# Two attention layers mixed by a gate: first loads from three queues, and the last rows' work shared among four engines

## The chip, the cores and the metric

The kernel runs on one core of one Trainium2 chip. The metric is the device time of one launch in microseconds (us); before the change it is 2832.03 us, the median of three runs (2831.45 to 2834.38). A core has a matrix engine (TensorE; PE in the profile, with PEld its weight loads), a vector engine (DVE), a scalar engine (ACT), a general engine (Pool) and a queue engine (SP) that only issues transfers. ACT and Pool can issue transfers too, in the order of their other work.

## The reference

Two attention layers read the same input and are mixed row by row by a gate. Layer A has 32 heads with keys and values of their own; layer B has 32 query heads and one shared key and value. S is 2048, D is 576, a head is 18 wide.

```python
x = A_x
g = _sigmoid((x * gate_w).sum(-1, keepdims=True))
a = _A_ref(x, A_wqkv, A_wo)      # full attention, 32 heads
b = _B_ref(x, B_wq, B_wk, B_wv, B_wo)   # 32 query heads, one key and value
return g * a + (1 - g) * b
```

Each layer is softmax(q k^T / sqrt(18)) v for every head, the heads side by side, times an output matrix of 576x576. So the output is one product: the 64 heads' rows, each divided by its softmax sum and multiplied by its gate, times the two output matrices stacked (1152x576).

## The kernel before

Numbers that need float32 precision are split into a high and a low part (`split`: a rounding copy, then a subtraction), and a product is made as high x high + high x low + low x high.

**First stage.** The input, transposed, comes in eight chunks `xs` of 256 columns (`load_x`), each by three transfers (`load5`: 512 KB and twice 64 KB). The projection weights come in 14 blocks `wst` of 128 columns (`load_w`, 256 KB and twice 32 KB). Before the change all of these are issued by SP in this order: block 0, chunks 0 to 3, block 1, chunks 4 to 7, blocks 2 to 5. A transfer uses one of eight semaphores in turn (eight more for Pool's queue), and its issue waits until the transfer that used it before has landed. ACT and DVE split each chunk (lines 210 to 212) and each weight block (lines 126 and 127); `project` multiplies on PE (line 147), and writes the results to DRAM (`qkh` from ACT's queue, `qkl` from Pool's). Blocks 0 and 1 are projected as chunks arrive, the others in `project_rest`.

**Main stage.** A loop over steps T gives every engine a hand-written order: for each of 64 heads and 16 blocks of keys, scores on PE (line 377), exponential on ACT (line 384), the weighted sum of values on PE into `acc` (line 391), and the row maxima of the heads to come on DVE (lines 342 to 351). Other work is pulled in at given steps: the normalising of finished rows (`normalise`, nine tiles of 128 rows) and the output product (`out_proj`, three parts, each 16 tiles of rows `st_` times two halves `hf` of 288 columns), which adds each half-tile into `oacc` on DVE (line 515; the first part is copied by ACT, line 513). A half-tile takes one of four PSUM buffers `pm`.

**The end.** The ninth tile of rows holds 110 rows and is normalised with `at_end`: four chunks of 512 columns, each a multiplication, a rounding copy and a subtraction on DVE (lines 447, 116, 118), left in `qs` and `ksb` for the third `out_proj`. The last head's 18 rows get a way of their own, `last_out`: ACT copies `acc` to `oe` and rounds it to `oh` (lines 536, 114), DVE makes the low part `ol`; 12 transfers stack `oh`, `oh` and `ol` into `qs[2]` (54 rows); PE transposes the sums and DVE makes `r` from them (lines 548 to 552). Then come the half-tiles of the third `out_proj` that are left (`pull(10 ** 9)`), and at last, for each of 16 tiles, two products of the stacked rows (line 558), each scaled by `r` and added to `oacc` by one DVE instruction (line 561), and a store of the tile to `out` (288 KB) by SP. SP's and all other transfers go through the helper on line 49.

The order at the end is this:

```python
    tail = last_out()
    next(tail)
    pull(10 ** 9)
    run(tail)
```

Of the kernel before, what the change touches and what calls it, by code (L numbers as in the profile page):

```python
# [8 lines left out]
F32 = mybir.dt.float32  # L9
F32R = mybir.dt.float32r  # L10
BF16 = mybir.dt.bfloat16
AF = mybir.ActivationFunctionType
OP = mybir.AluOpType
# [29 lines left out]
def gated_mix_kernel(ctx: ExitStack, tc: tile.TileContext, xT, wall, wv, wo, out):  # L43
    nc = tc.nc
    P = 128
# [71 lines left out]
        if l is not None:  # L117
            eng_l.tensor_tensor(l, src, h.bitcast(F32), op=OP.subtract)

    def load5(t, src):  # L120
        dma(t[:, 0:4, :], src[0:512, :].rearrange("(k p) m -> p k m", p=P))
        dma(t[0:64, 4, :], src[512:576, :])
        dma(t[64:128, 4, :], src[512:576, :])

    def split_w(st, w, eng_l):
        nc.scalar.activation(w["h"], st, AF.Copy)
        eng_l.tensor_tensor(w["l"], st, w["h"].bitcast(F32), op=OP.subtract)

    def load_w(mt):
        st = wpool.tile([P, NKT, P], F32, name="wst", bufs=6)  # L130
        load5(st, wall[mt])
        return st

    def prep_w(st):
# [61 lines left out]

    WV = []
    with tc.tile_pool(name="xs", bufs=6, side="right") as xsp:
        W = [load_w(0)]
        XS = []  # L200

        def load_x(c):
            XS.append(xsp.tile([P, NKT, 256], F32, name="xs"))
            load5(XS[c], xT[:, 256 * c:256 * c + 256])

        def split_x(c):
            xs = XS[c]
            cs = slice(c * 256, (c + 1) * 256)
            xh = X["h"][:, :, cs]
            nc.scalar.activation(xh, xs, AF.Copy)  # L210
            nc.vector.tensor_tensor(X["l"][:, :, cs], xs[:, 0:4], xh[:, 0:4].bitcast(F32), op=OP.subtract)
            nc.vector.tensor_tensor(xh[64:128, 4], xs[64:128, 4], xh[64:128, 4].bitcast(F32), op=OP.subtract)

        for c in range(4):
            load_x(c)
        W.append(load_w(1))
        for c in range(4, 8):
            load_x(c)
        for mt in range(2, 6):
            W.append(load_w(mt))  # L220
        WP = [prep_w(W.pop(0))]
        for c in range(2):
            split_x(c)
        WP.append(prep_w(W.pop(0)))
        for c in range(4):
            if c < 3:
                split_x(2 * c + 2)
                split_x(2 * c + 3)
            keep = project(0, c, WP[0])
            project(1, c, WP[1])  # L230
            shared_v(*keep)
# [64 lines left out]
    L = {("kd", 0): kdb}  # L296
# [120 lines left out]
    def normalise(t, at_end=False):  # L417

        u0 = 0 if t == 0 else last_head(t - 1) + 1
        u1 = min(last_head(t) + 1, NU - 1)  # L420
        rows = min(P, DH * (NU - 1) - P * t)
        n = (u1 - u0) * 16
        sm = L["work"].tile([P, P], F32, name="sm", bufs=1)
        dma(sm[:n, :], sum_d[u0:u1, :].rearrange("h (s f) -> (h s) f", f=P))
        gt = L["work"].tile([P, P], F32, name="gt", bufs=1)
        dma(gt[:n, :], gu_d[u0:u1, :].rearrange("h (s f) -> (h s) f", f=P))
        yield
        yield
        nc.vector.reciprocal(sm[:n, :], sm[:n, :])
        (nc.vector if at_end else nc.gpsimd).tensor_tensor(sm[:n, :], sm[:n, :], gt[:n, :], op=OP.mult)  # L430
        yield
        dma(r_d[u0:u1, :].rearrange("h (s f) -> (h s) f", f=P), sm[:n, :])
        yield
        ot = OT.pop(t)
        R = L["work"].tile([P, S], F32, name="R", bufs=1)
        r0 = P * t
        while r0 < P * t + rows:
            u = r0 // DH
            n = min(DH * (u + 1), P * t + rows) - r0
            dma(R[r0 - P * t:r0 - P * t + n, :], r_d[u:u + 1, :].to_broadcast([n, S]))  # L440
            r0 += n
        yield
        if at_end:
            L["end"] = {"h": qs[1], "l": L["ks"][2]}
            for c in range(4):
                cs = slice(512 * c, 512 * c + 512)
                nc.vector.tensor_tensor(ot[:rows, cs], ot[:rows, cs], R[:rows, cs], op=OP.mult)
                split(ot[:rows, cs], L["end"]["h"][:rows, cs], L["end"]["l"][:rows, cs], nc.vector, nc.vector)
            return
        for c in range(4):  # L450
            cs = slice(512 * c, 512 * c + 512)
            h = L["work"].tile([P, 512], F32R, name="oh", bufs=1)
            l = L["work"].tile([P, 512], F32R, name="ol", bufs=1)
            nc.gpsimd.tensor_tensor(ot[:rows, cs], ot[:rows, cs], R[:rows, cs], op=OP.mult)
            yield
            split(ot[:rows, cs], h[:rows], l[:rows], nc.gpsimd, nc.gpsimd)
            yield
            yield
            dma(on_d[0][P * t:P * t + rows, cs], h[:rows])
            dma(on_d[1][P * t:P * t + rows, cs], l[:rows])  # L460
            yield

    WO = {}

# [12 lines left out]
    def out_proj(t0, rows, first=False):  # L477

        nt = len(rows)
        oacc = L["oacc"]  # L480
        O = {}

        def load(q):
            for x, y in enumerate("hl"):
                if "end" in L:
                    O[q, y] = L["end"][y][:, 256 * q:256 * q + 256].rearrange("p (t s) -> p t s", t=1)
                    continue
                t = L["pool"].tile([P, nt, 256], F32R, name=f"oi{y}", bufs=2)
                dma(t, on_d[x][P * t0:P * (t0 + nt), 256 * q:256 * q + 256]
                    .rearrange("(t p) s -> p t s", p=P))  # L490
                O[q, y] = t

        load(0)
        yield
        w = WO[t0]
        for q in range(8):
            if q < 7:
                load(q + 1)
            o = {y: O[q, y] for y in "hl"}
            for s2 in range(2):  # L500
                st_ = 2 * q + s2
                for hf in range(2):
                    fp = ps_m.tile([P, 512], F32, name="pm")
                    n = 0
                    for a, b in PRODS:
                        for t, r in enumerate(rows):
                            nc.tensor.matmul(fp[:, 0:288], o[b][:r, t, s2 * P:(s2 + 1) * P],  # L507
                                             w[a][:r, t, 288 * hf:288 * hf + 288],
                                             start=(n == 0), stop=(n == 3 * nt - 1))
                            n += 1  # L510
                    dst = oacc[:, st_, 288 * hf:288 * hf + 288]
                    if first:
                        nc.scalar.activation(dst, fp[:, 0:288], AF.Copy)
                    else:
                        nc.vector.tensor_tensor(dst, fp[:, 0:288], dst, op=OP.add)  # L515
                    yield
# [17 lines left out]
    def last_out():  # L534
        oe = L["work"].tile([P, 512], F32, name="oe", bufs=1)
        nc.scalar.activation(oe, acc, AF.Copy)
        oh = L["work"].tile([P, 512], F32R, name="oh", bufs=1)
        ol = L["work"].tile([P, 512], F32R, name="ol", bufs=1)
        split(oe, oh, ol, nc.scalar, nc.vector)
        stk = qs[2]  # L540
        for j in range(4):
            cs = slice(512 * j, 512 * j + 512)
            dma(stk[0:18, cs], oh[32 * j:32 * j + 18, :])
            dma(stk[18:36, cs], oh[32 * j:32 * j + 18, :])
            dma(stk[36:54, cs], ol[32 * j:32 * j + 18, :])
        pt = ps_m.tile([P, 512], F32, name="pm")
        for c in range(4):
            nc.tensor.transpose(pt[:, P * c:P * c + P], oe[:, P * c:P * c + P], ident)
        r = L["work"].tile([P, 16], F32, name="rl")
        nc.vector.reciprocal(r.rearrange("p (j c) -> p c j", c=4),  # L550
                             pt.rearrange("p (c j d) -> p c j d", c=4, d=32)[:, :, :, 18])
        nc.vector.tensor_tensor(r, r, L["g"], op=OP.mult)
        oacc = L["oacc"]
        yield
        for st_ in range(16):
            for hf in range(2):
                ps = ps_m.tile([P, 512], F32, name="pm")
                nc.tensor.matmul(ps[:, 0:288], stk[0:54, st_ * P:st_ * P + P],
                                 L["wl"][0:54, 288 * hf:288 * hf + 288], start=True, stop=True)
                dst = oacc[:, st_, 288 * hf:288 * hf + 288]  # L560
                nc.vector.scalar_tensor_tensor(dst, ps[:, 0:288], r[:, st_:st_ + 1], dst,  # L561
                                               op0=OP.mult, op1=OP.add)
            dma(out[st_ * P:(st_ + 1) * P, :], oacc[:, st_, :])


    NSTEP = 16 * NU
# [80 lines left out]
        run(slow.pop(0))  # L647
    tail = last_out()
    next(tail)
    pull(10 ** 9)  # L650
    run(tail)

# [33 lines left out]
```

## Time and profile before

| | us |
|---|---|
| median of three runs | 2832.03 (2831.45 to 2834.38) |
| the profiled execution | 2830.23 |
| its span | 2828.1 |
| PE busy | 2801.4 (99%) |
| ACT busy | 2447.0 (87%) |
| DVE busy | 2371.8 (84%) |
| POOL busy | 207.6 (7%) |

The span runs from the first to the last instruction of the profiled execution, which took 2.13 us more than that. Busy time is the time in which an engine worked on instructions; issues of transfers, waits and register work don't count, except that Pool's own issues do. In a row of the timeline stand start, length, engine, line, operation, output and inputs, and how many instructions were merged; brackets give the idle time before it and what ended it. `SPq` is the issuing side of SP: the length of such a row is the time to issue, not to move the data. The matrix engine's clock is given as a share of full speed.

### The profile page before, as it was taken

The page shows a single profiled execution, that of the slowest core. Times are in us where ns is not written, and L with a number is a line of the kernel's source. Part 1 is how long each engine was busy: PE and PEld are TensorE (multiplying, and loading weights), DVE is VectorE, ACT ScalarE, POOL GpSimd, SP SyncE. Part 2 cuts the span into 40 slices and gives each one's busy share as a digit, 9 for nine tenths or more (in the row PEclk, how much of TensorE's full clock was granted, in tenths as well). Part 3 has the DMA queues.
Part 4 walks back from the last instruction along what each step waited for, and adds up shares of the span by engine and source line. Part 5 has one row for each costly group of instructions (what it writes and reads, how often), then busy time and mean ns, then how long its engine had stood idle before and what let it go on. Part 6 is the DMA issues. An engine that isn't in the chain of part 4 may idle for free.

```text
span 2828.1 us, 58626 instructions
## 1 busy us (share of the span) xinstructions
PE 2801.4 (99%) x22628; PEld 1289.3 (46%) x22628; DVE 2371.8 (84%) x4461; ACT 2447.0 (87%) x4832; POOL 207.6 (7%) x364
## 2 busy tenths in 40 slices
PE   7999999999999999999999999999999999999999
PEld 5888443343433433434434444444444444345554
DVE  3346999999999999999999888888888888998765
ACT  3331999999999999999999999999999999997775
POOL 2220000011001000100110001000100011011000
PEclk9999999999999999999999999999999999999998
DMA  8662011121112111211143233233232323243412
GB/s 251 236 222 71 25 29 32 32 57 46 38 26 60 45 32 34 70 40 30 44 107 92 69 84 94 60 84 82 73 84 75 80 68 86 59 104 97 101 35 91
DMA packets 137147, 215.16 MB, mean 76 GB/s; under 512 B 55437, under 2 KB 94301, under 8 KB 125182
## 3 DMA queue, kind: packets, MB, share of 16 engines
q1 hardware_dynamic: 116156, 168.13, 22.6%
q10 hardware_dynamic: 14120, 22.30, 2.2%
q0 software_dynamic: 6592, 20.99, 2.1%
q8 instruction: 178, 2.92, 0.4%
q14 instruction: 101, 0.83, 0.1%
HBM read 137.31 MB, written 64.77 MB: 71 GB/s over the span
## 4 chain that ended last, share of the span: by engine, by line
PE 95%; DMA 2%; DVE 1%; SPq 0%; issue 0%; ACT 0%; POOL 0%; DVEq 0%; ACTq 0%; POOLq 0%
PE ps L377 40%; PE acc L391 38%; PE pm L342 6%; PE ps L147 5%; PE pm L507 4%; PE ps L187 2%; DMA xs<-xT 1%; DVE oacc L561 0%; PE pm L377 0%; DMA ksb<-qkl 0%; SPq L49 0%; DVE oacc L515 0%; DMA qkh<-ph 0%; DMA vg<-v_d 0%; DMA qkl<-pl 0%; DMA ksa<-qkh 0%
## 5 line engine op out<-in xcount | busy, mean ns | idle before, releaser
L384 ACT ACTIVATE pt<-ps 128x512 f32<-128x512 f32 x4052 | 2111.6, 613 | 106.0 <-PE pm L342 37.5
L351 DVE TENSOR_REDUCE mx<-pm 128x1 f32<-128x512 f32 x3094 | 1902.0, 681 | 63.1 <-PE pm L342 53.7
L377 PE MATMUL ps<-qs,ksb 56*128 56x512 f32 x2688 | 905.3, 433 | 0.0
L342 PE MATMUL pm<-ksb,qs 54*128 54x512 f32 x2363 | 815.3, 440 | 0.2
L377 PEld LDWEIGHTS ps<-qs,ksb 56*128 56x128 f32 x2688 | 442.8, 184 | 657.5 <-ACT pt L384 628.8
L391 PE MATMUL acc<-pt,vg 128*19 128x256 f32 (+1 forms) x6144 | 591.3, 457 | 0.8 <-ACT oe L401 0.8
L391 PE MATMUL acc<-pt,vb 128*19 128x256 f32 (+1 forms) x6144 | 591.5, 457 | 0.0
L348 DVE CUSTOM_DVE_ANT_0 junk<-pm,xb 128x512 bf16<-128x512 f32 x501 | 345.9, 690 | 192.7 <-ACT xb L345 150.2
L377 PE MATMUL ps<-qs,ksa 56*128 56x512 f32 x1364 | 459.2, 435 | 0.0
L342 PE MATMUL pm<-ksa,qs 54*128 54x512 f32 x1232 | 431.1, 439 | 0.0
L342 PEld LDWEIGHTS pm<-ksb,qs 54*128 54x128 f32 x2363 | 377.4, 184 | 5.8 <-issue 3.4
L377 PEld LDWEIGHTS ps<-qs,ksa 56*128 56x128 f32 x1364 | 220.3, 184 | 318.9 <-ACT pt L384 295.4
L345 ACT ACTIVATE xb<-pm 128x512 f32<-128x512 f32 x501 | 312.7, 624 | 0.2 <-PE pm L342 0.2
L391 PEld LDWEIGHTS acc<-pt,vg 128*19 128x19 f32 x6144 | 104.3, 97 | 223.5 <-issue 214.5
L391 PEld LDWEIGHTS acc<-pt,vb 128*19 128x19 f32 x6144 | 104.2, 96 | 212.0 <-issue 204.7
L342 PEld LDWEIGHTS pm<-ksa,qs 54*128 54x128 f32 x1232 | 197.6, 184 | 0.2
L342 PE MATMUL pm<-kdb,qs 54*128 54x512 f32 x373 | 175.5, 471 | 0.4 <-DVE mx L351 0.3
L116 POOL CAST mh<-mt 128x32 fp32r<-128x32 f32 x64 | 13.5, 211 | 1723.8 <-DVE mt L359 1723.8
L150 ACT ACTIVATE ph<-ps 128x512 fp32r<-128x512 f32 x56 | 33.5, 597 | 99.6 <-PE ps L147 88.2
L156 DVE TENSOR_TENSOR pl<-ps,ph 128x512 fp32r<-128x512 f32 x56 | 38.5, 691 | 95.8 <-ACT ph L150 63.3
L147 PE MATMUL ps<-xh,wh 128*128 128x512 f32 x280 | 75.7, 401 | 18.9 <-ACT xh L210 13.7
L147 PE MATMUL ps<-xh,wl 128*128 128x512 f32 x280 | 73.4, 392 | 0.0
(99 smaller groups left out, 1346.6 us busy)
## 6 DMA issues: line engine op xcount, KB each, us to landing
qs<-qkh SPq DMA_DIRECT2D x244, 144.0 KB
qs<-qkl SPq DMA_DIRECT2D x122, 144.0 KB
qkh<-ph ACTq DMA_DIRECT2D x56, 256.0 KB
qkl<-pl POOLq DMA_DIRECT2D x56, 256.0 KB, 3.2
ksa<-qkh SPq DMA_DIRECT2D x88, 144.0 KB
onh<-oh SPq DMA_DIRECT2D x32, 256.0 KB
onl<-ol SPq DMA_DIRECT2D x32, 256.0 KB
oih<-onh SPq DMA_DIRECT2D x16, 512.0 KB
```

The costliest lines, as they stand in the source:

```text
L147: nc.tensor.matmul(fp, w[a][:kr, k, :], X[b][:kr, k, cs], start=(n == 0), stop=(n == len(PROJ) - 1))
L150: nc.scalar.activation(h, fp, AF.Copy)
L156: nc.vector.tensor_tensor(l, fp, h.bitcast(F32), op=OP.subtract)
L187: nc.tensor.matmul(fp[:, 0:288], X[b][:kr, k, st_ * P:(st_ + 1) * P], w[a][:kr, k, :], start=(n == 0), stop=(n == len(PROJ) - 1))
L342: nc.tensor.matmul(pm, qs[u % 3][b:b + 54, i * P:(i + 1) * P], k, start=True, stop=True)
L345: nc.scalar.activation(MX["x"], pm, AF.Relu)
L348: nc.vector.tensor_tensor_reduce(junk, pm, MX.pop("x"), 1.0, -3e38, op0=OP.add, op1=OP.max, accum_out=MX[u][:, i, c:c + 1])
L351: nc.vector.tensor_reduce(MX[u][:, i, c:c + 1], pm, axis=AX.X, op=OP.max)
L377: nc.tensor.matmul(ps, kst(u)[b:b + 56, i * P:(i + 1) * P], qs[u % 3][b:b + 56, c * 512:(c + 1) * 512], start=True, stop=True)
L384: nc.scalar.activation(pt, ps, AF.Exp, scale=SCALE)
L391: nc.tensor.matmul(acc[32 * j:32 * j + 19, a:b], v_of(u, i), PT[u, i, j][:, a:b], start=(i == 0), stop=(i == 15), skip_group_check=True)
L507: nc.tensor.matmul(fp[:, 0:288], o[b][:r, t, s2 * P:(s2 + 1) * P], w[a][:r, t, 288 * hf:288 * hf + 288], start=(n == 0), stop=(n == 3 * nt ...
```

## The change

In the first stage, weight block 0 is issued by ACT and block 1 by Pool, both before the chunks of the input; SP issues the chunks one after the other. In `normalise(at_end)` the second of four chunks is done by Pool. Of the 12 stacking transfers SP keeps four, ACT issues four and Pool four. In the half-tiles of the third `out_proj` that come after `last_out` has begun (20 of 32), every second one is added by a new function, `add_by_pool`: ACT copies the half-tile from PSUM to a `pt` buffer in SBUF (there are 12), and Pool adds it to `oacc`. In the last loop, the tiles 1, 4, 7, 10 and 13 go the same way, with ACT scaling by `r`, and Pool issues their stores; DVE and SP keep the 11 others.

```diff
-    def load5(t, src):
+    def load5(t, src, eng=None):
...
-        W = [load_w(0)]
+        W = [load_w(0, nc.scalar), load_w(1, nc.gpsimd)]
...
-        for c in range(4):
-            load_x(c)
-        W.append(load_w(1))
-        for c in range(4, 8):
+        for c in range(8):
             load_x(c)
...
             for c in range(4):
                 cs = slice(512 * c, 512 * c + 512)
-                nc.vector.tensor_tensor(ot[:rows, cs], ot[:rows, cs], R[:rows, cs], op=OP.mult)
-                split(ot[:rows, cs], L["end"]["h"][:rows, cs], L["end"]["l"][:rows, cs], nc.vector, nc.vector)
+                eng = nc.gpsimd if c == 1 else nc.vector
+                eng.tensor_tensor(ot[:rows, cs], ot[:rows, cs], R[:rows, cs], op=OP.mult)
+                split(ot[:rows, cs], L["end"]["h"][:rows, cs], L["end"]["l"][:rows, cs], eng, eng)
...
+    def add_by_pool(dst, fp, scale=1.0):
+
+        t = L["pt"].tile([P, 512], F32, name="pt")
+        nc.scalar.activation(t[:, 0:288], fp[:, 0:288], AF.Copy, scale=scale)
+        nc.gpsimd.tensor_tensor(dst, t[:, 0:288], dst, op=OP.add)
...
                     if first:
                         nc.scalar.activation(dst, fp[:, 0:288], AF.Copy)
+                    elif "over" in L and hf:
+                        add_by_pool(dst, fp)
                     else:
                         nc.vector.tensor_tensor(dst, fp[:, 0:288], dst, op=OP.add)
...
             dma(stk[0:18, cs], oh[32 * j:32 * j + 18, :])
-            dma(stk[18:36, cs], oh[32 * j:32 * j + 18, :])
-            dma(stk[36:54, cs], ol[32 * j:32 * j + 18, :])
+            dma(stk[18:36, cs], oh[32 * j:32 * j + 18, :], nc.scalar)
+            dma(stk[36:54, cs], ol[32 * j:32 * j + 18, :], nc.gpsimd)
...
-                nc.vector.scalar_tensor_tensor(dst, ps[:, 0:288], r[:, st_:st_ + 1], dst,
-                                               op0=OP.mult, op1=OP.add)
-            dma(out[st_ * P:(st_ + 1) * P, :], oacc[:, st_, :])
+                if st_ % 3 == 1:
+                    add_by_pool(dst, ps, r[:, st_:st_ + 1])
+                else:
+                    nc.vector.scalar_tensor_tensor(dst, ps[:, 0:288], r[:, st_:st_ + 1], dst,
+                                                   op0=OP.mult, op1=OP.add)
+            dma(out[st_ * P:(st_ + 1) * P, :], oacc[:, st_, :], nc.gpsimd if st_ % 3 == 1 else None)
...
     next(tail)
+    L["over"] = True
     pull(10 ** 9)
     run(tail)
```

More of the change, by code (lines that the diff above doesn't have):

```diff
@@ L118, in split @@
             eng_l.tensor_tensor(l, src, h.bitcast(F32), op=OP.subtract)
-    def load5(t, src):
-        dma(t[:, 0:4, :], src[0:512, :].rearrange("(k p) m -> p k m", p=P))
-        dma(t[0:64, 4, :], src[512:576, :])
-        dma(t[64:128, 4, :], src[512:576, :])
+    def load5(t, src, eng=None):
+        dma(t[:, 0:4, :], src[0:512, :].rearrange("(k p) m -> p k m", p=P), eng)
+        dma(t[0:64, 4, :], src[512:576, :], eng)
+        dma(t[64:128, 4, :], src[512:576, :], eng)
     def split_w(st, w, eng_l):
@@ L127, in split_w, with load_w @@
         eng_l.tensor_tensor(w["l"], st, w["h"].bitcast(F32), op=OP.subtract)
-    def load_w(mt):
+    def load_w(mt, eng=None):
         st = wpool.tile([P, NKT, P], F32, name="wst", bufs=6)
-        load5(st, wall[mt])
+        load5(st, wall[mt], eng)
         return st
```

## The prediction

> **What bounds the kernel now.** I read the page first, then the waits of PE, then the two ends by stretches and in order of time.
>
> ```profile
> span 2828.1 us, 58626 instructions
> PE 95%; DMA 2%; DVE 1%; SPq 0%; issue 0%; ACT 0%; POOL 0%; DVEq 0%; ACTq 0%; POOLq 0%
> ```
>
> The chain that ended last is 95% PE. The edit leaves PE's 22628 matmuls as they are, so it can only take time out of the two ends. The profiled execution took 2830.23 us, 2.13 us outside its span, and lies 1.80 us under the median of 2832.03; I carry differences over to the median unchanged.
>
> The start: PE's waits in all, then stretches (length, PE, PEld, DVE, ACT, POOL busy, clock, DMA share, GB/s).
>
> ```profile
> PE ps L147 <- ACT xh L210: 13.7, 1, 13.7
> PE ps L147 <- ACT wh L126: 4.4, 2, 3.8
> PE ps L147 <- DVE pl L156: 0.8, 1, 0.8
> ...
> 2.00:8.00 6.00, 0.00 (x0) 0.00 (x0) 0.00 (x0) 2.00 (x2) 0.17 (x1) 1.00 0.61 170
> 8.00:12.00 4.00, 0.00 (x0) 0.00 (x0) 2.42 (x3) 1.29 (x2) 0.00 (x0) 1.00 0.73 214
> 12.00:24.00 12.00, 9.74 (x35) 7.20 (x36) 5.77 (x8) 5.90 (x7) 0.00 (x0) 1.00 1.02 288
> 24.00:46.00 22.00, 20.24 (x95) 15.78 (x93) 13.04 (x22) 10.41 (x14) 4.58 (x8) 1.00 0.91 295
> 46.00:72.00 26.00, 21.96 (x84) 17.60 (x84) 4.96 (x8) 5.60 (x9) 10.69 (x21) 0.87 0.83 237
> 72.00:200.00 128.00, 127.78 (x563) 105.81 (x564) 49.76 (x70) 42.49 (x69) 33.00 (x62) 1.00 0.67 232
> ```
>
> PE waits 13.7 us for the first data. The DMA engines are full from 12 us (288 GB/s) but not before (170, then 214). After 72 us PE is never idle, so what is gained by then stays, and nothing later adds to it.
>
> The end, in order of time; first and last start of the stores' issues; two stretches with the columns above.
>
> ```profile
> 2801.53 1.54 SPq L49 DMA_DIRECT2D qs<-oh  x2
> 2802.34 0.68 DVE L118 TENSOR_TENSOR ol<-oe,oh 128x512 fp32r<-128x512 f32 x1
> 2803.31 7.68 DVE L515 TENSOR_TENSOR oacc<-pm,oacc 128x288 f32<-128x288 f32 x20
> 2810.43 13.12 PE L558 MATMUL pm<-wl,qs 54*128 54x288 f32 x32
> 2810.92 13.68 DVE L561 SCALAR_TENSOR_TENSOR oacc<-pm,rl,oacc 128x288 f32<-128x288 f32 x32
> 2811.88 13.08 SPq L49 DMA_DIRECT2D out<-oacc  x16
> ...
> L49 SPq DMA_DIRECT2D out<-oacc x16: 332/332/373, 2811.9 to 2824.6; - x16
> ...
> 2800.70:2811.00 10.30, 10.30 (x77) 9.91 (x75) 10.20 (x28) 0.72 (x2) 0.00 (x0) 1.00 0.17 41
> 2813.00:2826.00 13.00, 10.53 (x25) 6.81 (x24) 11.60 (x28) 0.00 (x0) 0.00 (x0) 0.50 0.93 348
> 2826.00:2828.10 2.10, 0.00 (x0) 0.00 (x0) 0.00 (x0) 0.00 (x0) 0.00 (x0) 0.50 0.12 45
> ```
>
> DVE is busy without a gap from 2803.31 to 2824.60, which looks like the bound. But up to 2811 PE is just as full (10.30 of 10.30), and from 2813 to 2826 the DMA engines are 0.93 busy with the 16 stores. Three resources end there within 2 us of each other.
>
> **The change, part by part.**
>
> *First loads.* W0 (three DMAs) leaves SP for ACT, whose first work was to wait for it; W1 leaves SP for Pool's queue.
>
> ```profile
> 2.23 1.75 SPq L49 DMA_DIRECT2D wst<-wall  x3
> 4.03 7.84 SPq L49 DMA_DIRECT2D xs<-xT  x12
> ...
> 11.91 3.18 SPq L49 DMA_DIRECT2D wst<-wall  x3
> 12.40 1.27 ACT L210 ACTIVATE xh<-xs 128x1280 fp32r<-128x1280 f32 x1 [2.06 <-DMA xs<-xT]
> ...
> 13.72 2.51 PE L147 MATMUL ps<-xh,wh 128*128 128x512 f32 x5 [13.72 <-ACT xh L210]
> ...
> 18.73 0.74 ACT L126 ACTIVATE wh<-wst 128x640 fp32r<-128x640 f32 x1 [5.05 <-DMA wst<-wall]
> ```
>
> x now starts at 2.23 instead of 4.03: 1.8 us. W1 (320 KB, 328 kB) was behind four chunks of x; now it runs beside the first two and costs them up to 328/288 = 1.1 us, so the low end is 0.7. The high end is the holes: 6 x 170 + 4 x 214 = 1876 kB by 12 us would take 6.5 us at 288, done by 9 instead of 12: 3.0. ACT's wait for W1 at 18.73, which held the next splits behind it, goes, and SP loses three issues there. I take 2.0, near the 1.8 that is simply read off. Pool's three issues have no row at that size; its issues of 256 KB take 0.55 (below), and its next work is at 25 us. If no part of the gain got through the full DMA stretch from 12 to 72 us it would be 0; if W1 came later than 18.7, a loss of its lateness.
>
> *Last rows' normalising.* One of four chunks goes to Pool.
>
> ```profile
> 2785.26 0.69 DVE L447 TENSOR_TENSOR ot<-ot,R 110x512 f32<-110x512 f32 x1 [10.41 <-DMA R<-r_d]
> 2786.45 0.69 DVE L118 TENSOR_TENSOR ksb<-ot,qs 110x512 fp32r<-110x512 f32 x1
> ...
> 2788.44 0.40 PE L507 MATMUL pm<-woh,qs 110*128 110x288 f32 x1
> ...
> 2792.43 0.81 DVE L515 TENSOR_TENSOR oacc<-pm,oacc 128x288 f32<-128x288 f32 x2
> 2794.18 0.46 DVE L515 TENSOR_TENSOR oacc<-pm,oacc 128x288 f32<-128x288 f32 x1 [0.94 <-PE pm L507]
> ```
>
> Four chunks are 7.17 us on DVE, so 1.8 us fewer; but the third addition waits 0.94 for PE, so DVE was early and the 1.8 is worth nothing. PE reads the second chunk only from output tile 4, its ninth half-tile, and the third half-tile's addition is at 2794.18: Pool has over 8.9 us for 3.2 (two at 1.29, one at 0.61, rows below). Cost 0; were that cover gone, PE would wait for Pool.
>
> The Trainium skill, SBUF — State Buffer, "Who interferes with whom", says that a DVE instruction with two SBUF inputs and a GpSimd one reading SBUF exclude each other for a whole instruction. No row here has such a pair. By that rule the first chunk, which PE waits for, would end late; that result is a rival below.
>
> *Stacking copies.* Twelve issues on SP become four each on SP, ACT and Pool. SP was through with them before its first store at 2811.88, and DVE never waited for them: no gain. But on ACT four at 0.77 (1.54/2) hold its queue from 2801.53 to 2804.6, and its new evictions wait behind them. PE does a half-tile of three matmuls in 3 x 10.30/77 = 0.40 us, so its 20 take 8.0 and began at 2810.43 - 8.0 = 2802.4. The sixth, due at 2804.4, needs the second's buffer (there are four), which ACT's first eviction (0.41, row below) frees at 2805.0: a new wait of 0.6 us on the path, between 0 (if ACT issues at the 0.33 of SP's stores) and 0.8.
>
> *Additions.* Pool cannot be seen adding 128x288, so by its neighbours (mean ns of one; then Pool in order of time):
>
> ```profile
> L454 POOL TENSOR_TENSOR ot<-ot,R 128x512 f32<-128x512 f32 x32 | 41.2, 1286 | 125.3 <-DMA qs<-qkh 29.4 <-DMA R<-r_d 26.6 <-DMA vg<-v_d 26.2
> L430 POOL TENSOR_TENSOR sm<-sm,gt 112x128 f32<-112x128 f32 x7 | 3.2, 458 | 212.3 <-DVE sm L429 212.3
> L49 POOL DMA_DIRECT2D qkl<-pl x56 | 30.6, 546 | 132.7 <-DVE pl L156 127.8 <-DVE vb L177 2.2 <-DMA wst<-wall 2.1
> L513 ACT ACTIVATE oacc<-pm 128x288 f32<-128x288 f32 x32 | 13.2, 412 | 38.5 <-PE pm L507 38.5
> ...
> 626.31 0.61 POOL L116 CAST oh<-ot 128x512 fp32r<-128x512 f32 x1
> 627.00 1.29 POOL L118 TENSOR_TENSOR ol<-ot,oh 128x512 fp32r<-128x512 f32 x1
> 628.24 1.30 POOL L454 TENSOR_TENSOR ot<-ot,R 128x512 f32<-128x512 f32 x1
> ...
> qkl<-pl POOLq DMA_DIRECT2D x56, 256.0 KB, 3.2
> ```
>
> (1286 - 458)/384 = 2.16 ns per element gives 0.80 us for 288, and 0.05 less from start to start (627.00 to 628.24): 0.76.
>
> Of the 20 additions left of the third product, ten go to ACT and Pool. DVE halves, but PE needs the same 8.0 us for its 20 half-tiles, plus the wait above: DVE's first last-row addition moves from 2810.92 to about 2811.4. DVE then has 22 of 32 at 13.68/32 = 0.43: ends 2820.8 instead of 2824.6.
>
> Pool: four copies from 2803.0 to 2805.2, ten additions paced by PE (0.8 a pair) to 2812.25, ten more at 0.76 and four stores at 0.62 in between, to 2822.3, where it issues its fifth store. That takes 1.7 us as SP's last (issued 2824.6, data until 2826.3, below) or 3.2 as Pool's own writes in the busy stretch: 2825.5, the later.
>
> Stores: 16 x 288 KB = 4.72 MB. At 348/0.93 = 374 GB/s this takes 12.6 us and no less, whoever issues it. Its data began at 2812.9, about 1.0 after the first issue, and ended at 2826.3 (the last stretch's 45 x 2.1 = 95 kB). Now it begins at 2813.4 and ends at 2826.0. So the store stream is the last of the three, and the end gains 0.3 to 0.4 us, where DVE alone would say 3.8.
>
> On the cap the Trainium skill speaks against the change too: DMA: Bandwidth & Descriptors, "Issuing engines are not separate DMA queues", has every queue on the same 16 engines, and its "Where 436 GB/s comes from" puts HBM at about 358 GB/s per core. By 358 the stores take 13.2 us and the end loses 0.2; the trace's 348 at 0.93 busy bears out a cap, but not which.
>
> Sum: -2.0 at the start, 0 at the normalising, -0.4 at the end: -2.4, so 2832.03 - 2.4 = 2829.6.
>
> **Rivals.**
> 1. *Pool and DVE exclude each other in the normalising.* DVE's second and third instruction on the first chunk would each stand behind one of Pool's (1.29, 0.61), 1.9 us. PE read that chunk at 2788.44, 1.3 us after its end at 2787.14: it would wait 0.6, and 1.0 with the starts falling badly: 2830.6. The rule named above speaks for it; no row against.
> 2. *Faster by more.* The start gains its 3.0 with PE's 3.8 us wait shortened too, and the stores, spread over two queues, exceed 374 GB/s so that the end goes by Pool's 2825.5 or DVE: -1.5 or more. 3.0 + 1.5 + 1.5 = 6.0: 2826.0. Against it: no stretch shows more than 348.
> 3. *The start does not carry.* The weights and writes of 12 to 72 us fill the DMA engines (0.83 to 1.02), and PE's 3.8 us wait grows by what was won: 0 and -0.4: 2831.6.
> 4. *Slower: Pool sets the end.* It has 0.5 us in hand (2825.5 against 2826.0). If each addition also waits out one DVE instruction (0.43), it needs 1.19 us: 2805.2 + 20 x 1.19 + 4 x 0.62 + 3.2 = 2834.7, 8.4 after the 2826.3 of before: 2832.0 - 2.0 + 8.4 = 2838.4. It decides from about 0.8 us an addition, and passes 0.2% at 1.15. Against it: 0.76 comes from two sizes, and DVE's operand there is half in PSUM.
>
> **How the numbers follow.** This measurement tells about 0.2% (5.7 us) from no change: under 2826.4 is faster, above 2837.7 slower. Forecast 0.53, rival 1 0.14, rival 2 0.13, rival 3 0.13, rival 4 0.07. The forecast and rivals 1 and 3 lie within 0.2%: 0.80; rival 2 is faster: 0.13; rival 4 slower: 0.07. The range 2826.0 to 2833.5 takes in 0 to 3.0 at the start, -1.5 to +1.5 at the end, and leaves out most of rival 4.
>
> **What would show it.** Right: PE's first matmul at 11 to 12.5 instead of 13.72; a wait of PE of about 0.7 for ACT near 2804; DMA share still 0.9 in the last 13 us, with DVE done 3 to 4 us before the last store's data; Pool's additions at 0.80. Wrong: the PE waits before 72 us grow (rival 3), a late first chunk (1), or Pool busy and its last store alone at the end (4).

## The result and the profile after

The changed kernel takes 2840.12 us (median of 11 runs, 2835.72 to 2844.38) beside 2832.63 us for the kernel before on the same chip (11 runs): a ratio of 1.0025, 95% interval 1.0016 to 1.0035. It is slower by 7.5 us, where 2.4 us less was predicted, and lies outside the predicted range.

The profiled execution took 2841.77 us. From its page the span and the chain, then PE's waits (us in total, times, longest), which answer to those shown of before:

```profile
span 2840.0 us, 58682 instructions
PE 96%; POOL 1%; DMA 1%; issue 1%; DVE 0%; ACT 0%; SPq 0%; POOLq 0%; ACTq 0%; DVEq 0%
...
PE ps L147 <- ACT xh L210: 13.2, 1, 13.2
PE ps L147 <- ACT wh L126: 3.1, 1, 3.1
PE ps L147 <- DVE pl L156: 3.0, 1, 3.0
```

PE's first data come 0.5 us earlier and its longest wait for weights is 0.7 shorter (3.1 instead of 3.8), but its wait for DVE has grown from 0.8 to 3.0. POOL now has a part in the chain that ended last.

The end, first Pool's part of the timeline, then two stretches (length, PE, PEld, DVE, ACT, POOL busy, clock, DMA share, GB/s):

```profile
2825.57 1.56 POOL L465 TENSOR_TENSOR oacc<-pt,oacc 128x288 f32<-128x288 f32 x2
2827.42 0.56 POOL L49 DMA_DIRECT2D out<-oacc  x1 [0.30 <-DVE oacc L570]
2828.00 1.54 POOL L465 TENSOR_TENSOR oacc<-pt,oacc 128x288 f32<-128x288 f32 x2
2829.84 0.56 POOL L49 DMA_DIRECT2D out<-oacc  x1 [0.30 <-POOL oacc L465]
...
2818.00:2832.20 14.20, 8.70 (x24) 5.84 (x23) 8.09 (x19) 3.78 (x8) 10.82 (x16) 0.51 0.88 331
2832.20:2840.00 7.80, 0.00 (x0) 0.00 (x0) 0.00 (x0) 0.00 (x0) 0.00 (x0) 0.50 0.00 0
```

The second stretch is the answer: for 7.8 us, to the end of the span, no engine works and no byte moves. What runs there isn't counted as busy. It is among the instructions of the program's last line (L692; L682 before), here of both kernels: durations in ns (shortest, median, longest), first and last start.

```profile
L682 POOLq DRAIN  x3: 40/102/8142, 2747.2 to 2827.8; - x3
L682 SPq DRAIN  x3: 7/7/7, 2827.2 to 2827.6; - x3
...
L692 POOLq DRAIN  x3: 46/106/9392, 2829.8 to 2839.7; - x3
L692 SPq DRAIN  x3: 7/7/7, 2832.8 to 2839.5; - x3
```

When an engine has no more work it executes a DRAIN, and the program ends when all engines are through with theirs. SP's comes after the last store has landed. Pool's lasts 8.14 us in the kernel before too, but begins at 2747.2, when Pool has done its last work, 80 us before anybody needs it. In the changed kernel it begins at 2829.8 and lasts 9.39: SP is through at 2832.8 and waits 6.4 us for Pool.

So the 11.9 us between the two spans fall into three parts. The last score matmuls show how far PE was behind when the end began:

```profile
L377 PE MATMUL pm<-qs,ksa x44: 388/494/500, 2745.0 to 2794.1; 56*128 56x512 f32 x44
...
L374 PE MATMUL pm<-qs,ksa x44: 388/492/500, 2749.9 to 2798.9; 56*128 56x512 f32 x44
```

PE is 4.8 us late there; SP's DRAIN is 5.6 late, so the end itself costs 0.8; and from SP's DRAIN to the end of the span it is 7.2 instead of 0.9: 6.3. The 4.8 arises far ahead of the end: PE's first score matmul starts at 284.9 us in both profiles (rows below), and soon after it the changed kernel's profile has a stretch that the profile of before happens not to have:

```profile
289.00:299.00 10.00, 10.00 (x49) 3.40 (x51) 6.79 (x13) 5.98 (x13) 0.00 (x0) 0.50 0.01 4
```

For 10.2 us the clock is granted at 0.50, and PE does 49 matmuls in these 10 us; in the profile of before it does 83 there, at a clock of 1.00. An idle time of PE of 0.30 us lies 3 us ahead of it (at 285.6), but the profile of before has the same one (0.31 us at 285.6) without such a stretch behind it, so what decides it isn't shown. Of the 17 profiles of this study 14 have a stretch of 3.4 to 10.2 us there, between 280 and 305 us, with the old and the new start; the profile of before is one of the three without. I therefore don't put the 4.8 down to the change; that the new start doesn't cost it is tested below. The Trainium skill, TensorE: Matmul & The Clock Gate, section "What's actually happening", tells of an activity window of 3.4 us that runs freely; that agrees with the lengths here, multiples of 3.41 us. The two parts that are left, 0.8 and 6.3, make 7.1, and the medians differ by 7.5.

### The profile page after: what moved, and what is told of

It reads as the page before. It is cut to its first block, busy times and chain, and to the rows that moved or that the text cites. A ratio compares the mean times of both kernels' runs of the same rounds, so it can differ in the third digit from the quotient of the medians.

```text
span 2840.0 us, 58682 instructions
## 1 busy us (share of the span) xinstructions
PE 2804.3 (99%) x22628; PEld 1289.6 (45%) x22628; DVE 2365.6 (83%) x4438; ACT 2456.3 (86%) x4852; POOL 233.4 (8%) x399
## 4 chain that ended last, share of the span: by engine, by line
PE 96%; POOL 1%; DMA 1%; issue 1%; DVE 0%; ACT 0%; SPq 0%; POOLq 0%; ACTq 0%; DVEq 0%
PE ps L374 40%; PE acc L388 38%; PE pm L339 6%; PE ps L147 5%; PE pm L511 4%; PE ps L187 2%; POOL oacc L465 1%; PE pm L374 0%; DMA ksb<-qkl 0%; DMA qkl<-pl 0%; DMA xs<-xT 0%; POOL qs L49 0%; SPq L49 0%; DVE mx L348 0%; POOL ksb L49 0%
## 5 line engine op out<-in xcount | busy, mean ns | idle before, releaser
L147 PE MATMUL ps<-xh,wh 128*128 128x512 f32 x280 | 75.6, 401 | 19.3 <-ACT xh L210 13.2
```

The lines of the kernel that those rows point to most:

```text
L147: nc.tensor.matmul(fp, w[a][:kr, k, :], X[b][:kr, k, cs], start=(n == 0), stop=(n == len(PROJ) - 1))
```

## Experiments on the end: Pool's DRAIN

Theory D: Pool's DRAIN is the cost. Rival A: Pool's additions and late stores are.

**All stores on SP** (of the changed kernel).

```diff
-            dma(out[st_ * P:(st_ + 1) * P, :], oacc[:, st_, :], nc.gpsimd if st_ % 3 == 1 else None)
+            dma(out[st_ * P:(st_ + 1) * P, :], oacc[:, st_, :])
```

> The changed kernel, except that all 16 stores of the output are issued by SP; Pool keeps its additions and its stacking copies. Theory D (the five stores that Pool issues make Pool's last DRAIN long: in the changed kernel's profile 9.39 us, 6.3 us more at the end of the program than before): the DRAIN on Pool is back at about 0.1 us, the program ends within 1 us of SP's last landing, and the time falls by about 6.4 us, from 2840.1 to about 2833.7. Rival A (Pool's additions and their place in the order of the stores set the end): the additions stay, so the time falls by 1 us at most, to about 2839. Should the DRAIN stay long without any store of Pool, it belongs to Pool's additions or to its stacking copies, and D falls.

Measured: 2836.15 us against 2833.12, ratio 1.0008 (0.9999 to 1.0017).

```profile
L692 POOLq DRAIN  x3: 46/106/9571, 2823.0 to 2833.0; - x3
L692 SPq DRAIN  x3: 7/7/7, 2830.1 to 2832.8; - x3
```

The DRAIN is about as long as in the changed kernel (9.57 against 9.39); it only begins sooner, since Pool has no stores to wait for. It ends at 2832.5, 2.4 us after SP's. So the DRAIN still sets the end, but not because of Pool's late stores: the theory's detail, that these stores make the DRAIN long, falls. The time fell by 4.0 us, where A allowed 1 at most; the small addition below decides between the two.

**Only the last store, or only the first, on Pool** (of the kernel before; `st_ == 15` and `st_ == 0`).

```diff
-            dma(out[st_ * P:(st_ + 1) * P, :], oacc[:, st_, :])
+            dma(out[st_ * P:(st_ + 1) * P, :], oacc[:, st_, :], nc.gpsimd if st_ == 15 else None)
```

> The kernel before, except that the last of the 16 stores, and it alone, is issued by Pool. Theory D (after a store of its own Pool's DRAIN lasts about 9.4 us from its issue): the store is issued at about the same time, lands some 3 us later, and Pool's DRAIN ends about 9.4 us after the issue, so the time grows by 6 to 7 us, to about 2839. Rival A (no such cost; a store by Pool is only somewhat slower in landing): 0.5 to 1 us more, about 2833.4.

> The kernel before, except that the first of the 16 stores, some 13 us ahead of the end, is issued by Pool. Theory D with a cost that runs from the issue of Pool's last store: it is over before the end, so the kernel before within 0.3 us, about 2832.6, with the DRAIN on Pool at 0.1 us or a few us, but not last. Theory D with a cost that is paid when the DRAIN comes, whenever the store was: again 6 to 7 us more, about 2839.

Measured: the last store 2838.66, ratio 1.0020 (1.0011 to 1.0029); the first 2832.09, 1.0001 (0.9992 to 1.0010). The row of the one, then of the other:

```profile
L682 POOLq DRAIN  x3: 46/102/8544, 2830.2 to 2839.3; - x3
...
L682 POOLq DRAIN  x3: 46/102/8546, 2813.3 to 2828.6; - x3
```

One store of 288 KB handed to Pool costs 5.5 us at the end and nothing that can be measured 13 us ahead of it; the DRAIN is equally long, and what counts is when it begins.

**One small addition on Pool as its last work, and the same without any transfer by Pool** (of the kernel before).

```diff
+        z = L["work"].tile([P, 16], F32, name="z", bufs=1)
+        nc.gpsimd.tensor_tensor(z, oacc[:, 15, 0:16], oacc[:, 15, 560:576], op=OP.add)
```

The second kernel also has, in the helper that issues every transfer:

```diff
-        return (eng or nc.sync).dma_start(o, i)
+        return (nc.sync if eng in (None, nc.gpsimd) else eng).dma_start(o, i)
```

> The kernel before, and as Pool's last work one small addition that nothing uses (128x16, of two slices of the last tile of the output, so it comes after DVE's last addition). No transfer of Pool is added: its last one is that of the first stage. Theory D2 (Pool's DRAIN takes 8 to 9.6 us after whatever instruction is Pool's last: 8.14 us at 2747 us in the kernel before, where it is hidden, 9.57 after the additions of the changed kernel with all stores on SP): the DRAIN begins near 2825 and ends 8 to 8.5 us later, and the time grows by 5.5 to 6.5 us, to about 2838.6. Theory D1 (only a late transfer of Pool makes it long): the kernel before within 0.5 us.

> As the one with the small addition of Pool at the end, and every transfer that Pool issues in the first stage is issued by SP instead, so Pool issues none in the whole program. If the DRAIN is long because Pool has issued transfers at all (its queue has to be wound up): the DRAIN is about 0.1 us, and the time is that of the kernel before, but for some us that the first stage may lose or gain by the move (seen in PE's starts). If it is long whatever Pool did: 8 us as without the move, and 5.5 to 6.5 us more than before at the end.

Measured: with the small addition 2837.93 against 2831.86, ratio 1.0017 (1.0008 to 1.0027); without transfers of Pool 2851.46, 1.0072 (1.0058 to 1.0086). Pool's and SP's rows of both:

```profile
L684 POOLq DRAIN  x3: 40/102/8106, 2830.7 to 2839.3; - x3
L684 SPq DRAIN  x3: 7/7/7, 2833.3 to 2839.0; - x3
...
L684 POOLq DRAIN  x3: 39/78/322, 2845.6 to 2848.2; - x3
L684 SPq DRAIN  x3: 7/7/7, 2847.7 to 2848.1; - x3
```

An addition of 0.22 us costs 6 us by the medians, and 2 to 8 by the interval of the ratio, because it puts off the DRAIN: A falls, and so does D1, which needs a late transfer. With no transfer by Pool in the whole program the DRAIN's row is 0.32 us long, the addition included. (That kernel is slower for another reason: SP's queue then holds the writes of the first stage as well, PE waits 17.3 us in all for DVE's `pl`, and PE's first score matmul comes at 306.5 instead of 284.9.) The DRAIN is thus the price of transfers that Pool issued 2.7 ms earlier. Before, there are 95 of them:

```profile
qkl<-pl POOLq DMA_DIRECT2D x56, 256.0 KB, 3.2
kdl<-pdl POOLq DMA_DIRECT2D x10, 256.0 KB, 3.9
qs<-qkh POOLq DMA_DIRECT2D x12, 144.0 KB, 6.5
...
```

(the other 17 in rows of 1 to 6). Counted in each trace from the end of Pool's last work to the end of its DRAIN:

| transfers issued by Pool | us |
|---|---|
| 0 | 0.07 |
| 95 (before; the small addition) | 7.85, 7.85 |
| 96 (one store) | 7.91 |
| 98 (the new start alone) | 8.09 |
| 102 (all stores on SP) | 8.42 |
| 107 (the changed kernel) | 8.81 |

That is 0.07 + 0.082 x the number, whatever their size and age: the four stacking transfers of 36 KB that lie between 98 and 102 added 0.33 us, the five stores of 288 KB between 102 and 107 added 0.39. The next kernel tests it.

**29 loads of the first stage issued by SP instead of Pool** (of the changed kernel; lines 237 to 240 and 253 of the kernel before, `ones_r` likewise).

```diff
-    load_k(ksb, ROW_KB, nc.gpsimd)
-    load_kd(kdb, ROW_KB, nc.gpsimd)
-    load_q(0, nc.gpsimd)
+    load_k(ksb, ROW_KB)
+    load_kd(kdb, ROW_KB)
+    load_q(0)
...
-                load_q(mt - 3, nc.gpsimd)
+                load_q(mt - 3)
```

> The changed kernel with 29 transfers of the first stage (the rows of keys and queries for the first heads) issued by SP instead of Pool, so Pool issues 78 in place of 107. Theory D3, the length of Pool's DRAIN goes by the number of transfers that Pool issued in the whole program: from the traces so far 0.065 us with none, 7.85 with 95, 8.09 with 98, 8.42 with 102, 8.81 with 107, counted from the end of Pool's last work, so 0.082 each; here 0.07 + 78 x 0.082 = 6.45, and the program ends 2.4 us earlier than the changed kernel against PE's work, about 2837.8. Rival (it goes by something else, the bytes or the time since): 8.4 to 8.8 as with 102 to 107.

Measured: 2833.33 against 2833.37, ratio 0.9999 (0.9990 to 1.0008).

```profile
L692 POOLq DRAIN  x3: 46/93/7028, 2821.9 to 2829.7; - x3
L692 SPq DRAIN  x3: 7/7/7, 2824.9 to 2829.5; - x3
```

From the end of Pool's last work the DRAIN takes 6.44 us; 6.45 was expected. By the medians the time fell by 6.8 us against the changed kernel, to 2833.3 where I expected about 2837.8, and only 2.4 of it are the DRAIN's. PE's first score matmul comes at 277.3 instead of 284.9, so the rest came from the start, to which I return.

## Experiments on the end: the stores

**Pool only on tiles 1 and 4 of the last loop, stores on SP** (of the changed kernel), so that the DRAIN is hidden.

```diff
-                if st_ % 3 == 1:
+                if st_ in (1, 4):
```

> The changed kernel with all stores on SP and, in the last loop, only tiles 1 and 4 added by Pool instead of five tiles. Theory D2: Pool's last addition comes some 9 us before the end, the DRAIN is hidden or sets the end by under 1 us, and the time is that of before or 1 us less: 2831.5 to 2833 (the changed kernel with all stores on SP and five tiles on Pool measured 1.0008 of before, some 2.3 us more). If Pool's backlog from the third product holds back the second store as it did there (issued 15.0 us after the last stacking transfer of before's clock, and the rest behind it), the last landing is still 1 us later than before against PE's work: 2833 to 2834.

Measured: 2832.89 against 2831.86, ratio 1.0005 (0.9997 to 1.0014). The DRAIN ends at 2825 and is hidden. PE's last score matmul comes at the same 2794.1 as in the profile of before, and SP's DRAIN still 1.0 us later. SP issued its first store at 2812.26 and the second at 2815.06: it stood behind Pool's additions to tile 1, which were behind ten additions of the third product. From then on:

```profile
2816.00:2826.00 10.00, 6.75 (x16) 4.32 (x16) 7.79 (x19) 0.00 (x0) 0.54 (x1) 0.50 1.02 386
```

The queued stores move at 386 GB/s, against 348 at a share of 0.93 before.

**An interleaved end, with Pool on tiles 1 and 4, then on 5 and 7; the latter also with the new start.** Start and normalising as before; of the stacking transfers ACT issues four and SP eight; all stores on SP; `last_out` yields after each tile.

```diff
-    pull(10 ** 9)
+    pull(16)
+    for st_ in range(16):
+        next(tail)
+        if st_ in (1, 3):
+            pull(2)
     run(tail)
```

> A version made to beat both: the first loads, the normalising and the stores (SP) as before; of the stacking transfers ACT issues four and SP eight; Pool adds ten half-tiles of the third product and those of tiles 1 and 4 of the last loop, so that it ends some 10 us before the end; and the last loop's tiles 0 to 3 come before the third product's tiles 14 and 15. By theory D2 the DRAIN on Pool ends near 2824 and is hidden. By the store stream (12.6 us of data) begun about 2.5 us earlier, SP's last landing comes 2 to 3.5 us earlier than before against PE's work: about 2830. If DVE or ACT sets the cadence instead, 0 to 1 us: about 2832.

> The interleaved end, with Pool on tiles 5 and 7 of the last loop instead of 1 and 4. In the version with 1 and 4, SP's store of tile 1 was issued 2.3 us after that of tile 0 and that of tile 4 again 2.3 after that of tile 3: SP stood behind Pool's additions, and the transfers stood still behind SP. If that is why the interleaved end gained nothing: the stores now follow one another in under 1 us, and SP's last landing comes about 2 us earlier than before against PE's work (12.2 us of data from about 2811), near 2830 in time. If it is not: SP's gaps go and the last landing stays within 0.5 us of before. The DRAIN on Pool ends 7.85 us after its last addition (95 transfers, as before) and is hidden either way.

> The interleaved end with Pool on tiles 5 and 7, together with the new first loads. If the two gains are there and add up (2 us at the end, 0.6 at the start by the run with the start alone): about 2829.4, against 2832 for the kernel before. If neither carries: 2832. The DRAIN on Pool 8.1 us after its last addition (98 transfers), hidden.

Measured: 2832.91, ratio 1.0002 (0.9993 to 1.0011); 2833.64, 0.9996 (0.9987 to 1.0005); 2832.07, 0.9995 (0.9987 to 1.0004). With Pool on 5 and 7 the stores go out 0.4 to 1.3 us apart, and once 1.7, so the long gaps are gone, and yet SP's DRAIN comes only 0.3 us earlier than before against PE's last score matmul (0.6 in the one with the new start, 0.1 with Pool on 1 and 4). I expected 2. So the standstill behind Pool was worth 0.2 us here, not 2. The last stores are 0.85 us apart, the pace of DVE's two additions a tile, and DVE is busy for 6.89 of the 7 us from 2823 on: it is the bound there, as before. None of these versions gains anything that can be measured.

## Experiments on the start

**The new start alone**, and **weight block 0 alone on ACT** (both of the kernel before).

```diff
-        W = [load_w(0)]
+        W = [load_w(0, nc.scalar), load_w(1, nc.gpsimd)]
...
-        for c in range(4):
-            load_x(c)
-        W.append(load_w(1))
-        for c in range(4, 8):
+        for c in range(8):
             load_x(c)
```

```diff
-        W = [load_w(0)]
+        W = [load_w(0, nc.scalar)]
```

> The kernel before with the change of the first loads alone (W1 ahead of x, weights issued by ACT and Pool). My prediction's term: 2830.6, that is 2.0 us less than before. Rival 3 (the start does not carry: what PE gains by 69 us is given back at a wait for DVE): the kernel before within 0.7 us, 2832 to 2833.3. Rival C (the new start brings the stretch of half clock at 289 us that the changed kernel's profile shows, which cost 4 us there): about 2836.5, with a stretch of PE at half clock near 289 us in this profile as well.

> The kernel before with one thing changed: weight block 0 is issued by ACT instead of SP; block 1 stays on SP behind chunk 3. My prediction's step: x then starts 1.8 us earlier, and block 1, which costs the first two chunks up to 1.1 us when it runs beside them, is out of the way, so PE's first matmul comes at about 11.9 (13.0 to 13.7 in the profiles with the old start, 12.5 to 13.2 with the new). If the transfers of the first chunks are bound by something else than their issue: 12.8 to 13.5. In time within 2 us of before either way.

Measured: the new start 2831.91 against 2833.12, ratio 0.9998 (0.9990 to 1.0007); block 0 alone 2830.51 against 2833.37, 0.9990 (0.9981 to 0.9999). PE's first matmul comes at 12.75 and at 11.28 us (12.9 to 13.7 in the profiles with the old start, 12.5 to 13.2 with the new). So, by single profiles, 2 us can be won there, and block 1 beside the first chunks takes 1.5 of them back, as my first step had it with 1.1. Block 0 alone is also faster in time, by 0.3 to 5.4 us. But the first score matmul, which ends the first stage, doesn't follow in the profiles:

```profile
L377 PE MATMUL ps<-qs,ksb x2688: 383/395/505, 284.9 to 2713.0; 56*128 56x512 f32 x192
...
L374 PE MATMUL ps<-qs,ksb x2688: 383/395/792, 284.9 to 2717.9; 56*128 56x512 f32 x192
...
L374 PE MATMUL ps<-qs,ksb x2688: 383/395/792, 286.9 to 2719.5; 56*128 56x512 f32 x192
```

These are before, the changed kernel and the new start alone: 284.9, 284.9, 286.9; block 0 alone has 285.9. With Pool issuing the loads named below, the profiles with the old start lie at 283.2 to 289.3, those with the new one at 281.5 to 287.1: the spread is wider than what is looked for. (The longest of these matmuls, 792 ns against 505, is the half clock right behind it.)

Rival C was that the new start brings this half clock and loses 4 us by it. Kernels with the old start have it too, though for a shorter time in single profiles (0 to 6.8 us in six, against 6.8 to 10.2 in five with the new start). All the runs decide: the granted clock, averaged over the program, is 0.9958 in the mean of eleven runs with the new start alone and 0.9955 in 33 runs of the kernel before. It isn't lower, so C falls.

Where an earlier start can be lost is seen in Pool's queue of the changed kernel, in what DVE waits for from 40 to 75 us (before, then changed), and in PE's wait behind that (before, then changed):

```profile
47.03 1.04 POOL L49 DMA_DIRECT2D ksb<-ones_r  x2
...
55.56 0.50 POOL L49 DMA_DIRECT2D qs<-qkh  x1 [1.22 <-DMA ksb<-qkl]
58.03 0.50 POOL L49 DMA_DIRECT2D qs<-qkh  x1 [1.97 <-DMA ksb<-qkh]
...
62.50 1.65 POOL L49 DMA_DIRECT2D qkl<-pl  x3
...
DVE pl L156 <- DMA qkl<-pl: 8.3, 2, 8.2
DVE pl L156 <- DMA qkl<-pl: 10.5, 1, 10.5
...
72.22 1.45 PE L147 MATMUL ps<-xh,wh 128*128 128x512 f32 x5 [0.77 <-DVE pl L156]
70.72 2.50 PE L147 MATMUL ps<-xh,wh 128*128 128x512 f32 x5 [3.05 <-DVE pl L156]
```

From 47 to 62.5 us Pool issues 17 loads, and waits for landings between them. Three writes of `pl` stand behind, no buffer `pl` comes free, DVE waits 10.5 us for one (8.2 before) and PE 3.0 for DVE. Work that arrives there earlier waits longer. And behind the longer wait come 3.4 us of half clock (70.5 to 73.9 us) that before doesn't have there: PE's 200th matmul starts at 64.8 us in the changed kernel against 68.6, its 250th at 81.0 in both. (Most of the 3.8 between 64.8 and 68.6 isn't the start's either: the profile of before has 6.8 us of half clock from 48 us on, the changed kernel's none there.) With block 0 alone the first matmul comes 2.4 us earlier than in the profile of before and the 250th 1.0 later, at 82.0 (79.2 to 85.4 in the profiles with the old start).

**The 29 loads on SP**, the edit shown above: alone, with block 0 on ACT, and with the whole new start; the end as before in all three.

> The kernel before with one thing changed: the 29 transfers that load the first heads' rows of keys and queries are issued by SP instead of Pool (they stand in Pool's queue from 47 to 64 us, each behind a landing, and the writes of pl behind them). Theory S (that queue takes up what the start wins: DVE finds no free pl, and PE waits for DVE): PE's wait for DVE pl goes, and PE is 2 to 5 us earlier at its 1200th matmul than the profiles with the old start (262.9 to 269.1), near 260; the time falls by 2 to 5 us, to about 2829. If it was not that queue: 263 to 269 and no change in time.

> Weight block 0 issued by ACT, and the 29 loads of the first stage issued by SP; all else as before. Theory S: the 2 us that block 0 alone won at PE's first matmul (11.28 against 13.0 to 13.7) now come through, so PE's 1200th matmul is about 2 us ahead of the kernel with the 29 loads alone, and the time is about 2 us under it: 2826 to 2828. If the start is taken up somewhere else before 264 us, the two are the same.

> The changed kernel's start (block 0 by ACT, block 1 by Pool) and the 29 loads issued by SP; the end as before. In the changed kernel with fewer transfers of Pool PE's 1200th matmul came at 257.1, 7.6 us ahead of the changed kernel's; here the same, 256.5 to 258, and without that kernel's DRAIN at the end the time is 5 to 7 us under before, unless the half clock near 290 us takes some of it: 2826 to 2829.

Measured against 2831.97 us: the loads alone 2827.81, ratio 0.9982 (0.9974 to 0.9991); with block 0 on ACT 2825.71, 0.9975 (0.9964 to 0.9985); with the new start 2825.24, 0.9980 (0.9971 to 0.9989). The loads alone, then with block 0; the last row is PE's wait for weights in the second. PE has no wait for DVE's `pl` left in any of the three:

```profile
L377 PE MATMUL ps<-qs,ksb x2688: 383/395/792, 279.6 to 2711.9; 56*128 56x512 f32 x192
...
L377 PE MATMUL ps<-qs,ksb x2688: 383/395/792, 278.4 to 2709.0; 56*128 56x512 f32 x192
...
PE ps L147 <- ACT wh L126: 2.2, 2, 1.5
```

The first score matmul comes 5.3 and 6.5 us earlier than in the profile of before (3.6 with the new start, at 281.3). Theory S holds: PE's wait is gone, and the time fell as it said. In the twelve profiles with these loads on Pool, PE takes 11.3 to 18.2 us from its 200th matmul to its 250th, and waits 0.7 to 4.2 us there for DVE's `pl` in eleven of them; in the four with these loads alone on SP it takes 11.3 or 11.4 and doesn't wait. Freeing Pool's queue is worth 4.2 us by itself. That the first loads then add 2 us more is what the medians say (2.1 with block 0, 2.6 with the whole new start; 2.0 and 0.6 by the ratios), but the intervals overlap, so it isn't settled. I expected PE's 1200th matmul 2 us ahead of the loads alone with block 0, and at 256.5 to 258 us with the new start; it came 1.2 ahead (257.8 against 259.0) and at 260.7, so the second was a miss. Block 0 on ACT with the loads on SP beats both kernels: 6.3 us under the one before, and some 14 under the changed one.

## Why the prediction was wrong

The forecast was 2829.6, the result 2840.1.

*The end's sum stopped too early.* The step that failed is the one under Additions that follows Pool "to 2822.3, where it issues its fifth store" and to that store's landing at 2825.5, and ends there. After an engine's last work comes its DRAIN, and Pool's is long. Cost of what was left out: 6.3 us. It could have been read: the row with 8142 ns at 2747.2 stands in the profile of before, where it is hidden behind 80 us of other work. The change moved Pool's last work from 2747 to 2829.8, and I asked for the work moved, its waits and issues, not for what follows an engine's last instruction. Rival 4, that Pool sets the end, named the right engine, and its 2838.4 came near by luck: its mechanism, additions at 1.19 us, was wrong. They took 0.80, 0.76 apart, as predicted:

```profile
L465 POOL TENSOR_TENSOR oacc<-pt,oacc 128x288 f32<-128x288 f32 x20 | 15.3, 805 | 0.1
```

*The stores: -0.4 predicted, +0.8 measured.* The step that failed is that the store stream is the last of the three and Pool has 0.5 us in hand: Pool was the last. The chain that ended last runs through Pool alone from its stacking transfers on, and Pool works without a gap:

```profile
2810.68 9.14 POOL oacc L465 x12
```

Its fifth store was issued at 2829.8, which is 2825.0 on before's clock (the 4.8 us taken off), instead of 2822.3. Of the 2.7 us, 1.2 come from the ten additions of the third product, which by this row end at 2818.3 (2813.5 on before's clock) instead of 2812.25; 1.5 come from the five stores, each of which waits 0.30 for its own additions to end (the timeline above), so that two additions and a store take 2.43 us (2825.57 to 2828.00) instead of 2.14. The data of Pool's last store end at 2832.2; those of SP's last store end at 2831.2, which is 2826.4 on before's clock, as before the change. The store stream was bound neither by 374 GB/s nor by the other cap: it moves 386 GB/s when stores queue up, above the 358 that the Trainium skill's DMA: Bandwidth & Descriptors, "Where 436 GB/s comes from", gives for a core's memory. It wasn't kept full: the share was 0.88 from 2818 to 2832.2. Why DVE, PE and ACT kept a pace of 2.47 us for three tiles there was not isolated.

*The start: -2.0 predicted.* With the new start alone it is -0.6, between -2.8 and +2.0, so how much of the 2.0 arrives isn't settled; nor do the profiles settle it, in whose mean the first score matmul comes 1.8 us earlier with the new start (284.4 against 286.3), spread over 6 us. What they show is that two steps were wrong. "I take 2.0" was too much already at PE's first matmul: it comes 0.5 us earlier, near the 0.7 that the sum had as its low end. The reading of the issue was right (2 us with block 0 alone), and block 1 beside the first chunks takes 1.5 of it back, where the sum had 1.1 at most. And the sum has no term for what stands between the first data and 72 us: the writes of `pl` behind Pool's loads can take up an earlier start. That PE isn't idle after 72 us held; what was lost in the changed kernel's profile was lost just ahead of that, and in the half clock behind PE's wait. Rival 3 had this, at the wrong wait: PE's 3.8 us for the weights shrank to 3.1, and the 0.8 for DVE, which I quoted and passed over, grew to 3.0.

*The stacking copies: a wait of 0.6 predicted.* Right. ACT's four issues held its evictions, and PE's half-tiles are 0.44 us later, as seen where the last loop begins:

```profile
2806.35 3.25 ACTq L49 DMA_DIRECT2D qs<-oh  x4
2809.64 1.01 ACT L464 ACTIVATE pt<-pm 128x288 f32<-128x288 f32 x3 [3.33 <-DMA qs<-oh]
```

*The normalising: 0 predicted.* Right in price, but only just; rival 1 was right in mechanism. DVE's and Pool's rows of the changed kernel:

```profile
2790.57 1.39 DVE L116 CAST qs<-ot 110x512 fp32r<-110x512 f32 x1
2791.99 0.98 DVE L118 TENSOR_TENSOR ksb<-ot,qs 110x512 fp32r<-110x512 f32 x1
2792.89 1.77 DVE L445 TENSOR_TENSOR ot<-ot,R 110x512 f32<-110x512 f32 x1
...
2789.88 1.79 POOL L445 TENSOR_TENSOR ot<-ot,R 110x512 f32<-110x512 f32 x1 [37.21 <-DMA R<-r_d]
2792.51 1.60 POOL L118 TENSOR_TENSOR ksb<-ot,qs 110x512 fp32r<-110x512 f32 x1
```

Beside each other both are slowed: 1.39 for a copy that takes 0.43 alone, 1.77 and 0.98 for 0.69, and on Pool 1.79 and 1.60 for 1.29. The rule of the Trainium skill, SBUF — State Buffer, "Who interferes with whom", on instructions with two SBUF inputs agrees with that for the 1.77 and 0.98; the copy, slowed most, reads one input. The first chunk is ready at 2792.97, 1.0 us later on before's clock, and PE reads it at 2793.25: of its 1.3 us in hand 0.3 were left.

## What to carry to other kernels

Ask of every engine what follows its last instruction, not only what it does last: if Pool has issued transfers anywhere in the program, let its last work end 0.07 us + 0.08 us for each of them ahead of the end (that is what it took here), or give those transfers to other queues. And before an earlier start is counted as a gain, follow it through every wait that stands behind it, the small ones too; here a queue that waited for landings in order stood in the way, and taking 29 loads out of that queue was worth more than the whole change was meant to win (4.2 us against 2.4).

## What the runs showed of the hardware beyond what I expected

- Pool's DRAIN at the end of the program lasts 0.07 us plus 0.082 for each transfer that Pool issued in the whole program: 0.07 with none, 5.48 with 66, 6.44 with 78, 7.85 with 95, 8.81 with 107. A transfer issued by Pool 2.7 ms before the end counts like one at the end. SP's, after 1523 transfers in the kernel before, lasts 0.01 us.
- Stores from SP alone, when they queue up, move 386 GB/s at a DMA share of 1.02 (10 us of the version with Pool on tiles 1 and 4); the 348 GB/s of the kernel before was DVE's pace of 0.85 us a tile of 288 KB.
